# Spacing the turnings and reordering the join's side work in a chain of expert blocks

## The chip, the cores and the metric

The kernel runs on one core of one Trainium2 chip. The metric is the device time of one execution in microseconds (us). Unless said otherwise, times are medians of several executions. All executions of one comparison ran on the same chip.

## The reference, cut to what matters

```python
# first: a linear attention with a per-channel decay w, state (D x D) per head
for t in range(S):
    y[:, :, t] = einsum('bhd,bhde->bhe', rt, state + u*k*v)
    state = w * state + einsum('bhd,bhe->bhde', kt, vt)
# then: a mixture of 8 experts; x is the attention's output, (4*768, 384)
e = argmax(x @ w_gate)              # or the expert of the token before, if sigmoid(x @ w_local) >= 0.5
out[token] = softmax(logits)[e] * (relu(x[token] @ w1[e]) @ w2[e])     # 384 -> 1024 -> 384
```

Everything is float32. Each token goes to one expert, so the kernel sorts tokens by expert, gathers their rows, and works one block of rows for one expert at a time.

## The kernel before

The experts' part is a chain of ten blocks. Blocks 0 and 1 take 192 rows each. Blocks 2 to 9 take 448, 424, 392, 376, 352, 336, 232 and 192 rows. A block has eight hidden steps `m`; each is three matrix products with w1 (six matmul instructions in the trace), followed by ScalarE's relu into `hT`. Blocks of 336 rows and more ("seven") use a Strassen-like scheme on their first 256 rows: after every second hidden step, seven products instead of eight. VectorE prepares four `sums` of hT and four `factors` of w2 for them. At the block's end a `join` of seven VectorE operations puts the results together. The rows beyond 256 are the "rest" and have a PSUM bank of their own.

"Turning" means that TensorE transposes gathered rows into a PSUM bank and VectorE copies them out (`exT`). "Sending" is the way back: transposing the result `yT`, scaling it on VectorE, and scattering it. From block 2 on, both share one bank.

```python
def run(self, att, flag, ready):
    ...
    for i in range(n):
        u = self.units[i]
        if EARLY <= i and i + 1 < n:
            self.fetch(i + 1, self.nc.sync)
            self.gather(i + 1)
        after = len(self.units[i + 1]["rows"]) if i + 1 < n else 0
        for m in range(FK):
            self.hidden(i, m)
            ...
            if sends and (m >= 1 if i > EARLY else i == EARLY and m >= 4):
                self.send(*sends.pop(0))
            if u["seven"]:
                if m % 2:
                    self.sums(i, m // 2)
                    self.seven(i, m // 2)
                    if m < FK - 1:
                        self.factors(i, m // 2 + 1)
            elif m and i == n - 1:
                self.rows(m - 1)
            elif m:
                self.output(i, m - 1)
            if i <= EARLY:
                self.routing(i * FK + m)
            ...
            if FK - after <= m:
                self.turn(i + 1, m - (FK - after))
        if i + 1 < n and self.units[i + 1]["seven"]:
            self.factors(i + 1, 0)
            self.both = False
        if u["seven"]:
            self.join(i)
            ...

def join(self, i):
    ...                                        # p(k): product k in its bank
    nc.scalar.copy(one, p(1))
    nc.vector.tensor_tensor(u6, p(6), one, op=Alu.add)
    nc.vector.tensor_tensor(c[0][:, :half], p(2), one, op=Alu.add)
    ...                                        # four more
    nc.vector.tensor_tensor(c[0][:, half:], p(3), u6, op=Alu.add)
    for x in range(2):
        self.scaled(i, x, c[x], c[x])          # ScalarE: times the gate; then a scatter
    if n <= P or n == P + HALF:
        self.scaled(i, 2, u["y"][:, :D], ...)  # the rest bank, the same way
        ...
    else:
        nc.scalar.copy(u["yT"]..., u["y"]...)  # the rest bank, to be sent in the next block

def routing(self, s):                          # s counts hidden steps from block 0 on
    ...
    if s == 2 * FK:
        r.ends(bank("tb2"))                    # the router's end: 28 small VectorE operations
    if s == 2 * FK + 4:
        self.flag(bank("fp"))                  # the decay count: four VectorE ops, a 1x1 matmul, three more
```

There are two PSUM banks `h` for the hidden step, five `yo` tiles for results on the way out, and six tiles for gathered rows.

## Time and profile before

| | before |
|---|---|
| time, three executions | 410.75, 410.84, 412.0 us |
| span of the profiled execution | 408.3 us |
| TensorE, VectorE, ScalarE, GpSimd busy | 94, 47, 20, 35% |
| block 2's first hidden matmul starts | 155.58 us |
| last block's first half-row matmul starts | 398.06 us |

A row of the time order gives the start, the busy time, the engine, line, operation and tiles, and in brackets the idle time just ahead of it with what ended that. Read a row such as `[1.33 <-ACT hT L1066]` as a question: why did ScalarE make hT so late? The rows that carry the argument stand in the prediction.

### The profile page before, as it was taken

What the parts mean: (1) busy time and instruction counts of PE and PEld (TensorE: products, weight loads), DVE (VectorE), ACT (ScalarE), POOL (GpSimd) and SP (SyncE); (2) the same over time, 40 slices, a digit from 0 to 9 for tenths busy, and PEclk for the clock granted to TensorE, in tenths of its full rate; (3) what the DMA queues carried; (4) which work ended last, traced back from release to release, by engine and by line L of the source; (5) the groups of instructions that cost most, each with busy time, mean ns of one, the idle gap of its engine ahead of it and who ended that gap; (6) DMA issues with size and microseconds to landing.
All of it is one profiled execution on the core that took longest, in us unless ns stands there. A gap on an engine that the chain in (4) does not pass through costs nothing. (4 is left out here: it accounts for less than half of the span.)

```text
span 408.3 us, 8809 instructions
## 1 busy us (share of the span) xinstructions
PE 384.6 (94%) x3616; PEld 298.5 (73%) x3616; DVE 191.5 (47%) x533; ACT 80.4 (20%) x195; POOL 143.8 (35%) x179
## 2 busy tenths in 40 slices
PE   7999999999999999989899999989989989989992
PEld 6777787777779996656587767867757757769972
DVE  7887667788744616343332342462343344230201
ACT  4122322222222111111211121120130121121110
POOL 8679998874210250021150051033014004013011
PEclk9999999999999999999999999999999999999998
DMA  7999999994139847013630461172083072072011
GB/s 257 410 413 408 410 384 318 319 382 182 27 102 357 323 120 309 0 30 104 250 110 0 155 232 43 35 314 73 2 315 100 2 307 87 2 303 86 2 34 35
DMA packets 17473, 74.94 MB, mean 184 GB/s; under 512 B 2735, under 2 KB 6592, under 8 KB 14865
## 3 DMA queue, kind: packets, MB, share of 16 engines
q1 hardware_dynamic: 10048, 56.89, 36.4%
q0 software_dynamic: 3424, 9.54, 7.4%
q10 hardware_dynamic: 3952, 7.87, 5.2%
q8 instruction: 30, 0.49, 0.5%
q14 instruction: 19, 0.15, 0.1%
HBM read 64.85 MB, written 9.54 MB: 182 GB/s over the span
## 5 line engine op out<-in xcount | busy, mean ns | idle before, releaser
L1061 PE MATMUL h<-exT,w1t 128*128 128x192 f32 (+7 forms) x480 | 138.2, 429 | 2.9 <-DVE exT L1048 2.9
L1061 PEld LDWEIGHTS h<-exT,w1t 128*128 128x128 f32 x480 | 85.3, 190 | 35.6 <-issue 12.7
L1176 POOL DMA_INDIRECT out_dram<-yo,sid x27 | 27.0, 1001 | 197.6 <-ACT yo L1171 131.0
L1066 ACT ACTIVATE hT<-h 128x192 f32<-128x192 f32 (+6 forms) x64 | 26.8, 428 | 140.9 <-PE h L1061 140.9
L1048 DVE COPY exT<-tp 128x384 f32<-128x384 f32 (+7 forms) x29 | 14.3, 494 | 68.0 <-PE tp L1047 68.0
L1034 POOL DMA_INDIRECT xg<-x_d,gid x29 | 29.8, 1027 | 45.7 <-DVE sm L873 25.8
L1084 DVE TENSOR_TENSOR sums<-hT 128x128 f32<-128x128 f32 x40 | 11.5, 288 | 60.3 <-ACT hT L1066 60.3
L288 DVE TENSOR_TENSOR am<-pair,kept 128x768 f32<-128x768 f32 x32 | 30.1, 952 | 13.8 <-PE pair L286 13.3
L220 POOL TENSOR_TENSOR pd<-rk 128x384 f32<-128x384 f32 x32 | 31.7, 1011 | 3.1 <-PE y L267 2.1
L1074 PE MATMUL y<-hT,w2t 128*128 128x192 f32 (+1 forms) x144 | 29.3, 340 | 1.2 <-ACT hT L1066 1.2
L1106 PE MATMUL y<-factors,sums 128*128 128x192 f32 x144 | 27.4, 327 | 0.7 <-DVE sums L1084 0.7
L295 PE MATMUL y<-am,kv 128*64 128x128 f32 x384 | 27.3, 278 | 0.8 <-DVE y L271 0.6
L1074 PEld LDWEIGHTS y<-hT,w2t 128*128 128x128 f32 x144 | 24.9, 190 | 2.0 <-ACT hT L1066 1.6
L216 POOL TENSOR_TENSOR ke<-kv,endT 128x288 f32<-128x288 f32 x32 | 24.9, 796 | 4.2 <-DMA kv<-in_kv_dram 3.2
L233 POOL TENSOR_TENSOR rw<-rk,tab 128x384 f32<-128x384 f32 x26 | 23.5, 923 | 4.8 <-PE y L308 4.8
L295 PEld LDWEIGHTS y<-am,kv 128*64 128x64 f32 x384 | 23.6, 136 | 1.6 <-DVE y L271 1.2
L1106 PEld LDWEIGHTS y<-factors,sums 128*128 128x128 f32 x144 | 24.0, 190 | 1.0 <-DVE sums L1084 1.0
L286 PE MATMUL pair<-rw,kw 48*64 48x128 f32 (+1 forms) x768 | 22.5, 249 | 1.2 <-ACT end L167 0.6
L1113 PE MATMUL tp<-w2t,hT 128*120 128x384 f32 (+2 forms) x48 | 19.7, 491 | 2.8 <-ACT hT L1066 2.8
L286 PEld LDWEIGHTS pair<-rw,kw 48*64 48x64 f32 x768 | 19.4, 133 | 2.7 <-issue 1.0
L312 ACT COPY xT<-y 128x768 f32<-128x768 f32 (+1 forms) x16 | 12.5, 779 | 38.7 <-PE y L308 38.7
L1106 PE MATMUL y<-w2t,hT 128*128 128x192 f32 x80 | 19.6, 326 | 0.0
(255 smaller groups left out, 501.5 us busy)
## 6 DMA issues: line engine op xcount, KB each, us to landing
w1t<-in_w_dram SPq DMA_DIRECT2D x9, 1536.0 KB, 6.2
w2t<-in_w_dram SPq DMA_DIRECT2D x9, 1536.0 KB, 7.1
rk<-in_rk_dram SPq DMA_DIRECT2D x15, 768.0 KB, 9.7
kv<-in_kv_dram SPq DMA_DIRECT2D x16, 584.0 KB, 9.3
vT<-in_vT_dram SPq DMA_DIRECT2D x16, 384.0 KB, 7.7
x_d<-x ACTq DMA_DIRECT2D x4, 1152.0 KB, 9.3
w1t<-in_w_dram ACTq DMA_DIRECT2D x1, 1536.0 KB, 9.0
w2t<-in_w_dram ACTq DMA_DIRECT2D x1, 1536.0 KB, 12.3
```

Source lines behind the costliest of these rows:

```text
L216: nc.gpsimd.tensor_mul(t["ke"][:, p::2], t["k"][:, p::2], spread(self.endT[:, p, hp], 1, C2))
L220: nc.gpsimd.tensor_mul(t["pd"][:, z], t["rT"][:, z], t["kT"][:, z])
L233: engine.tensor_mul(t["rw"][:, z], t["rT"][:, z], spread(pw, 1, z.stop - z.start))
L286: nc.tensor.matmul(sc[f * DP:(f + 1) * DP, h, i, x:], lhsT=t["kw"][q, c, o * DP:(o + 1) * DP], rhs=t["rw"][q, c, x:], start=True, stop=True)
L288: return lambda: nc.vector.tensor_mul(t["am"][:, g], sc, spread(self.kept[:, g:g + 3], 1, 2))
L295: nc.tensor.matmul(t["y"][p * DP:(p + 1) * DP, h, c2 * P:(c2 + 1) * P], lhsT=t["v"][:, (2 * c + h) * DH:(2 * c + h) * DH + DP], rhs=t["am" ...
L1034: self.nc.gpsimd.indirect_dma_start(out=xg[:n], out_offset=None, in_=self.x_d[:rows], in_offset=bass.IndirectOffsetOnAxis(ap=u["gid"][:n, ...
L1061: nc.tensor.matmul(h[:, :n], lhsT=u["w1"][:, m, kk, :], rhs=u["xT"][:, kk, :], start=(kk == 0), stop=(kk == DK - 1))
L1066: nc.scalar.activation(u[m], h[:, :n], Act.Relu)
L1074: nc.tensor.matmul(u["y"][d][:, :n], lhsT=u["w2"][:, m, d * P:(d + 1) * P], rhs=u[m], start=(m == 0), stop=(m == FK - 1))
L1106: nc.tensor.matmul(bank[:, x * half:(x + 1) * half], lhsT=a, rhs=b, start=(j == 0 and x == 0), stop=(j == FK // 2 - 1), skip_group_check=True)
L1176: self.nc.gpsimd.indirect_dma_start(out=out.rearrange("n (h d) -> (n h) d", h=2) if half else out, out_offset=bass.IndirectOffsetOnAxis(ap ...
```

## The change

Its intent is to close TensorE's holes around the borders of the large blocks, without changing any arithmetic.

```diff
 # join: the rest bank is emptied first
         nc.scalar.copy(one, p(1))
+        if n <= P or n == P + HALF:
+            self.scaled(i, 2, u["y"][:, :D], ...)
+        else:
+            nc.scalar.copy(u["yT"]..., u["y"]...)
         nc.vector.tensor_tensor(u6, p(6), one, op=Alu.add)
 ...
         for x in range(2):
             self.scaled(i, x, c[x], c[x])
-        if n <= P or n == P + HALF:
-            self.scaled(i, 2, ...)
-        else: ...
 # routing: the decay count moves ahead and is split, the router's end moves back by a step
-        if s == 2 * FK:
-            r.ends(bank("tb2"))
-        if s == 2 * FK + 4:
-            self.flag(bank("fp"))
+        if s == 13:
+            self.flag(0)
+        if s == 14:
+            self.flag(1, bank("fp"))
+        if s == 2 * FK + 1:
+            r.ends(bank("tb2"))
+            self.flag(2)
 # run
-                self.gather(i + 1)                       # at the block's start
+            lag = 2 if i and self.units[i - 1]["seven"] and i < n - 1 else 1
             for m in range(FK):
                 self.hidden(i, m)
-                if sends and (m >= 1 if i > EARLY else i == EARLY and m >= 4):
-                    self.send(*sends.pop(0))
                 if u["seven"]:
-                    if m % 2:
+                    if m % 2 == 0:
+                        if sends and (i > EARLY or m >= 4):
+                            self.send(*sends.pop(0))
+                    else:
+                        if m // 2 >= FK // 2 - after:
+                            self.turn(i + 1, m // 2 - (FK // 2 - after))
                         self.sums(i, m // 2)
                         self.seven(i, m // 2)
 ...
+                else:
+                    if sends and m >= 1 and i > EARLY:
+                        self.send(*sends.pop(0))
 ...
-                elif m:
-                    self.output(i, m - 1)
+                    elif m >= lag:
+                        self.output(i, m - lag)
-                if FK - after <= m:
+                if not u["seven"] and FK - after <= m:
                     self.turn(i + 1, m - (FK - after))
-            if i + 1 < n and self.units[i + 1]["seven"]:
-                self.factors(i + 1, 0)
+            if EARLY <= i + 1 and i + 2 < n:
+                self.gather(i + 2)                       # at the block's end
             if u["seven"]:
                 self.join(i)
 ...
+            if i + 1 < n and self.units[i + 1]["seven"]:
+                self.factors(i + 1, 0)
```

## The prediction

> **What bounds the kernel now.** I read the page first, then the list of waits, then the order of time from 108 us on, for TensorE alone and for all engines around the block borders.
>
> ```profile
> span 408.3 us, 8809 instructions
> PE 384.6 (94%) x3616; PEld 298.5 (73%) x3616; DVE 191.5 (47%) x533; ACT 80.4 (20%) x195; POOL 143.8 (35%) x179
> PEclk9999999999999999999999999999999999999998
> ```
>
> TensorE (PE) is busy 94% at full clock; no other engine passes half. So the time is TensorE's stream plus its holes, and only the holes can be won, as the change keeps every matmul. The chain of waits on the page is only the last scatter (1 us) and says nothing, so I looked for holes directly. The experts' part starts at 117 us with two blocks of 192 rows. Then come six blocks with seven products (448 to 336 rows; I call them blocks 2 to 7, from 155.6 us to 362 us) and two small ones, 8 (232 rows) and 9. Each border between the large blocks looks like this one, from block 5 to 6:
>
> ```profile
> 299.46 0.41 PE L1047 MATMUL tp<-ident,xg 96*128 96x96 f32 x3
> 299.91 0.46 DVE L1048 COPY exT<-tp 128x288 f32<-128x288 f32 x1 [2.23 <-PE tp L1047]
> 300.29 0.35 DVE L1092 TENSOR_TENSOR factors<-w2t 128x192 f32<-128x192 f32 x1
> 300.43 3.82 PE L1061 MATMUL h<-exT,w1t 128*128 128x352 f32 x12 [0.55 <-DVE exT L1048]
> 301.49 0.35 DVE L1148 TENSOR_TENSOR t<-y,t 128x192 f32<-128x192 f32 x1
> 303.20 0.35 DVE L1154 TENSOR_TENSOR yo<-mp,t 128x192 f32<-128x192 f32 x1
> 303.58 1.12 ACT L1171 ACTIVATE yo<-yo,gate 128x384 f32<-128x384 f32 x2 [5.23 <-DVE yo L1154]
> 304.61 0.56 ACT L1171 ACTIVATE yo<-tp,gate 120x384 f32<-120x384 f32 x1
> 305.07 0.80 ACT L1066 ACTIVATE hT<-h 128x352 f32<-128x352 f32 x2
> 305.57 0.89 PE L1113 MATMUL tp<-w2t,hT 128*96 128x384 f32 x2 [1.33 <-ACT hT L1066]
> ...
> 316.33 3.71 PE L1061 MATMUL h<-exT,w1t 128*128 128x352 f32 x12
> 319.88 0.81 PE L1113 MATMUL tp<-w2t,hT 128*96 128x384 f32 x2
> ```
>
> (The last two lines are from TensorE's own order of time.) Two holes are to be seen. First, the block's last turning ends in an exT copy for which the next block's first matmul waits, 0.55 us. Second, VectorE makes four factors, then seven join operations; ScalarE scales two tiles, then empties the rest bank, and only then comes the first hT, for which TensorE waits 1.33 us. Undisturbed, twelve hidden matmuls take 3.55 us from start to start (316.33 to 319.88); here they took 5.14. I measure losses this way, start to start, since a hole in a pipelined stream costs more than its idle entry says.
>
> Block 2 has three more, and the border to block 8 a large one:
>
> ```profile
> 163.32 1.24 PE L1106 MATMUL y<-factors,sums 128*128 128x192 f32 x6 [0.69 <-DVE sums L1084]
> 176.79 0.19 PE L1429 MATMUL tp<-r_ones,some 128*1 128x1 f32 x2 [1.24 <-DVE some L1428]
> 177.22 0.55 PE L1047 MATMUL tp<-ident,xg 128*128 128x128 f32 x3 [0.24 <-DVE over L1430]
> 187.54 0.55 PE L1047 MATMUL tp<-ident,xg 128*128 128x128 f32 x3 [0.71 <-DVE yo L1221]
> 363.05 2.62 PE L1061 MATMUL h<-exT,w1t 128*128 128x232 f32 x12 [0.57 <-DVE exT L1048]
> 366.89 1.44 PE L1074 MATMUL y<-hT,w2t 128*128 128x232 f32 x6 [1.23 <-ACT hT L1066]
> ```
>
> In block 2 the sums come late because the router's end (some 35 small operations) stands ahead of them on VectorE; the decay count makes TensorE wait twice; and a turning right behind a sending needs the one turning bank that VectorE still reads.
>
> **What the Trainium skill says.** "Perfetto Trace Analysis", section Optimization Strategy: find the gaps on the engine that binds, ask which semaphore ends them, and let that dependency start sooner; this trace names exT, hT, sums and some. "PSUM — Partial Sum Buffer", section Engine vs sequencer instructions: the Vector and Scalar queues are strict FIFO and matmuls start in program order. The border above agrees: hT at 305.07 us needs nothing from the join, but stands behind 1.5 us of scaling. So the place in the queue is the cost, and moving instructions is worth time. The same page, section PSUM bank collisions: engines are to be kept apart by bank, which is why a turning waits 0.71 us for the yo read of the same bank.
>
> **The change part by part.** No operation is added or removed except by place; the built order shows the same TensorE instructions.
>
> Turnings apart: in seven-product blocks each turning now stands after an odd hidden step and before the sums and products. The last exT copy (0.46 us) lies under some 3.2 us of products, and a hidden step of 2 us separates each turning from a sending. This takes away the first hole: turning to first hidden, start to start, against 0.33 us in mid-block: 0.42 us (block 3), 0.29, 0.78, 0.65, 0.57, 0.70 (block 8), together 3.4. In block 2 it takes away 187.54 minus 186.34, less 0.33, so 0.9.
>
> Rest bank first, factors after the join: let M be the start of the last product (299.14 at the border shown). The join's first operation needs product 7, which ends near M+0.2. It took 2.09 us from there to ScalarE's first scaling (301.49 to 303.58) and 1.03 us for the two scalings. The emptied rest bank (0.46 us) moves ahead, where ScalarE is idle. So hT starts at M+3.3 instead of M+5.9, and TensorE can use it 0.5 us later, at M+3.8. TensorE itself comes there at M+0.33 plus twelve hidden matmuls: 4.27 us for 424 rows, 3.95, 3.79, 3.55, 3.39 (336), so at M+4.6 down to M+3.7. The wait is gone up to 352 rows and about 0.1 at 336. The losses before, twelve matmuls' start to start less those times and the 0.1 of refill behind them: 1.36, 0.91, 0.98, 1.68, 1.81 us, together 6.7. About 6.6 of it goes. For blocks 4 and 5 this includes the sending's wait for yT, whose copy now lies before the join.
>
> Block 8: with two outputs' lag the third hidden step comes before the first output. But there are two h banks, so that step waits for the same first hT. TensorE is there at M+0.33+2.34, that is M+2.7; the bank is free near M+3.7. I expect 1.05 us to stay of 1.61, so 0.55 won, and the lag itself worth nothing.
>
> Router's end and decay count: the count's test is made two steps ahead, so neither the matmul nor the turning behind it waits: 175.05 to 177.22 is 2.17 us, less 0.33 for the sending and 0.1 for the matmul, so 1.7. The router's end now stands behind the first sums: 163.32 minus 162.14, less 0.33, plus refill, 0.95. It took VectorE 4.8 us (158.15 to 162.98). In the new place exT and sums of the next step follow. TensorE gives 4.5 us of hidden work, 0.3 of turning and 2.3 us of products before it needs them, 7.1 against 4.8+0.6+0.3. It fits with some 1 us to spare.
>
> Gathers: they go to GpSimd before the join's scatters. Turnings now start at the second hidden step, but the gathers for block 3 ended at 151 us already, and later ones get a whole block. This is needed for the turnings and wins nothing.
>
> The sum: 3.4 + 0.9 + 6.6 + 0.55 + 1.7 + 0.95 = 14.1 us. All of it is on TensorE's stream, and nothing waits for something else than that stream between 155 and 398 us. 410.8 less 14.1 is 396.7; I add half a microsecond for waits not seen, 397.2 us, 3.3% less.
>
> **The rivals.** One: the wait moves instead of going. VectorE's order has exT ahead of sums, so a product could wait for its sums, above all in block 2 behind the router's end, and the join's scatters now follow three or four gathers of 1.3 us each (1.0 and a 0.3 gap), so a yo buffer could come free late. Against it: the sums have 2.3 us of products ahead of them, and the five yo buffers come round only after most of a block (over 20 us). It would leave 2 to 4 us, some 400 us. Two: the join chain stays the bound. If VectorE's first join operation had to wait for the last product (M+0.5) or the scalings slipped, each of blocks 6 to 8 would keep 0.3 to 0.5 us more, 398.5 us. Three: the holes were filled anyway, as weights or the clock bind. Against it: weight transfers land 7 us after issue in blocks of 30 us, and the clock is already full (0.996); TensorE shows no wait for a transfer in this part. It would give 408 us or more.
>
> **Range and chances.** The sum rests on durations from the trace, each with a few tenths of error, and more can go wrong than can go better than nearly all of the holes closed. So 395.2 to 400.5 us. 2% faster is 402.6 us, reached if 58% of the sum comes. Faster 0.94, within 2% 0.05, slower 0.01.
>
> **What would show it.** TensorE's waits should list no exT, no some or over, no yo and no sums of note; only hT at block 8 near 1 us, and perhaps 0.1 at block 7. TensorE busy stays 384 us or a little less while the span falls to about 395 us, and its share rises to 97%. At each border the first hT should start 3.3 us after the last product's start. I would be wrong if product 5 waits for sums in every large block, if TensorE waits for gathers at the second hidden step, or if hT still comes 5 us or more after the last product.

## The result, and the profile after

The changed kernel took 397.66 us (median of four executions, 396.65 to 398.36) beside 411.42 for the kernel before (four, 410.75 to 414.32). The ratio is 0.9651, with a 95% interval of 0.9597 to 0.9704. It is the mean time of one kernel's fast runs over that of the other's of the same rounds, so it is not quite the ratio of the two medians. Later, on another occasion and with more rounds, it was 0.9671 (0.9640 to 0.9702).

The head of the page, and TensorE's list of waits (total, times, longest; waits of 0.4 us and less left out):

```profile
span 396.6 us, 8820 instructions
...
PE 382.4 (96%) x3616; PEld 298.0 (75%) x3616; DVE 190.4 (48%) x533; ACT 81.1 (20%) x195; POOL 144.5 (36%) x179
```

```profile
PE pair L151 <- POOL ident masks.py:199: 1.6, 1, 1.6
PE y L308 <- issue: 1.2, 1, 1.2
PE h L1061 <- ACT hT L1066: 1.0, 1, 1.0
PE y L295 <- DVE y L271: 0.6, 2, 0.4
PE pair L286 <- ACT end L167: 0.6, 1, 0.6
```

TensorE's busy time is almost what it was (384.6 before); its holes are gone. Of the waits named in the prediction one is left, for hT at block 8. The others listed lie in the attention part, which the change does not touch. The border from block 5 to 6 now:

```profile
292.37 0.59 ACT L1172 ACTIVATE yo<-tp,gate 120x384 f32<-120x384 f32 x1
...
293.25 0.49 PE L1106 MATMUL mp<-w2t,sums 128*128 128x192 f32 x2
...
293.53 0.36 DVE L1154 TENSOR_TENSOR t<-y,t 128x192 f32<-128x192 f32 x1 [1.95 <-PE y L1106]
293.58 3.71 PE L1061 MATMUL h<-exT,w1t 128*128 128x352 f32 x12
...
295.25 0.34 DVE L1160 TENSOR_TENSOR yo<-mp,t 128x192 f32<-128x192 f32 x1
...
295.63 1.12 ACT L1172 ACTIVATE yo<-yo,gate 128x384 f32<-128x384 f32 x2 [2.67 <-DVE yo L1160]
...
296.65 0.44 ACT L1066 ACTIVATE hT<-h 128x352 f32<-128x352 f32 x1
...
297.15 0.89 PE L1113 MATMUL tp<-w2t,hT 128*96 128x384 f32 x2
```

The last product starts at 293.25 us, and the next block's hidden matmuls follow 0.33 us later with no turning between. The rest bank is emptied before the last product even starts. The first hT comes 3.40 us after the last product's start (5.93 before), and TensorE goes on at 297.15, which is 3.57 us after its first hidden matmul: undisturbed would be 3.55.

Block 8 keeps its hole:

```profile
351.67 2.51 PE L1061 MATMUL h<-exT,w1t 128*128 128x232 f32 x12
355.13 1.44 PE L1061 MATMUL h<-exT,w1t 128*128 128x232 f32 x6 [0.95 <-ACT hT L1066]
```

**A measure without the attention part.** Block 2 began at 155.58 us in the one trace of the kernel before and at 157.82 us in the first one of the changed kernel. In the thirteen traces it ranged from 155.58 to 163.72 us, although the attention code is the same in all. In the first pair 1.97 of the 2.24 us were there before any experts' code: TensorE stood idle for 1.24 us at 60 us and again near 73 us, for no wait that the profile shows. I therefore read the **stretch** from block 2's first hidden matmul to the last block's first half-row matmul: 242.48 us before (398.06 minus 155.58), 228.48 us after (386.30 minus 157.82), so 14.0 us less. The decay count's 1x1 matmul now stands just outside it and costs little: from the last of the summing matmuls to block 2 it is 9.46 us (148.36 to 157.82) against 9.19.

### The profile page after: what moved, and what is told of

Read it like the earlier page. It is cut to its first block, busy times and chain, and to the rows that moved or that the text cites.

```text
span 396.6 us, 8820 instructions
## 1 busy us (share of the span) xinstructions
PE 382.4 (96%) x3616; PEld 298.0 (75%) x3616; DVE 190.4 (48%) x533; ACT 81.1 (20%) x195; POOL 144.5 (36%) x179
## 5 line engine op out<-in xcount | busy, mean ns | idle before, releaser
L1106 PEld LDWEIGHTS y<-w2t,hT 128*128 128x128 f32 x80 | 14.2, 190 | 7.0 <-issue 2.7
```

What stands on the lines that cost most here:

```text
L1106: nc.tensor.matmul(bank[:, x * half:(x + 1) * half], lhsT=a, rhs=b, start=(j == 0 and x == 0), stop=(j == FK // 2 - 1), skip_group_check=True)
```

## The experiments

Eleven runs were made, ten variants and the changed kernel once more as a control, all with correct results. Whole times moved by 1% between occasions (the kernel before: 411.4 to 415.4 us), so each is compared as a ratio to the kernel before of its own occasion, and by the stretch of its one profiled execution.

| label | what it is | ratio to before (95%) | stretch us | against changed |
|---|---|---|---|---|
| (changed) | first traced run | 0.9651 (0.9597 to 0.9704) | 228.48 | |
| turns_at_end | turnings late | 0.9828 (0.9782 to 0.9874) | 233.72 | +5.24 |
| rest_last | rest bank emptied last | 0.9843 (0.9783 to 0.9902) | 235.47 | +6.99 |
| factors_first | factors ahead of the join | 0.9707 (0.9648 to 0.9766) | 228.48 | 0.00 |
| gathers_late | gathers behind the scatters | 0.9859 (0.9798 to 0.9920) | 234.80 | +6.32 |
| count_back | decay count in block 2 | 0.9712 (0.9675 to 0.9748) | 230.13 | +1.65 |
| ends_back | router's end a step sooner | 0.9700 (0.9671 to 0.9729) | 229.64 | +1.16 |
| lag_one | block 8 without the lag | 0.9653 (0.9610 to 0.9697) | 228.50 | +0.02 |
| turns_end_factors_first | two parts undone | 0.9881 (0.9842 to 0.9920) | 237.48 | +9.00 |
| after_again | changed kernel, control | 0.9671 (0.9640 to 0.9702) | 228.50 | +0.02 |
| scale_later | scalings behind two hT steps | 0.9626 (0.9587 to 0.9665) | 226.94 | -1.54 |
| scale_later_lag_one | the same without the lag | 0.9652 (0.9611 to 0.9693) | 226.93 | -1.55 |

The control repeats the stretch within 0.02 us, so differences of a few tenths in this column mean something, where the whole times cannot show them.

### Turnings late

```diff
-                        if m // 2 >= FK // 2 - after:
-                            self.turn(i + 1, m // 2 - (FK // 2 - after))
                         self.sums(i, m // 2)
...
-                if not u["seven"] and FK - after <= m:
+                if FK - after <= m:
                     self.turn(i + 1, m - (FK - after))
```

> The changed kernel with its turnings put back to the last four (or three, or two) hidden steps, behind the sums and products; all else as changed. My theory (the gains add, each hole is its own): the exT copy stands before each next block again, 3.4 us over six borders, and in block 2 the two sendings at steps 4 and 6 are again followed at once by a turning in the same bank, 0.87 us each, 1.7 us: 5.1 us slower than the changed kernel, some 402.5 us. TensorE lists about 2.9 us of idle ended by exT again. Rival (the join chain was the only real bound, the turnings free once it is short): under 1.5 us slower.

The stretch grew by 5.24 us. TensorE's order of time at the border from block 5 to 6:

```profile
300.63 0.41 PE L1047 MATMUL tp<-ident,xg 96*128 96x96 f32 x3
301.60 3.82 PE L1061 MATMUL h<-exT,w1t 128*128 128x352 f32 x12 [0.55 <-DVE exT L1048]
305.25 0.81 PE L1113 MATMUL tp<-w2t,hT 128*96 128x384 f32 x2
```

The exT hole is back, and no hT hole follows. The latter is worth a thought: the late copy delays the join too, but it delays TensorE's own arrival as much (the join starts 1.15 us after the last product's start instead of 0.28, the next hidden step 1.29 us after it instead of 0.33). The two clashes in block 2 were 0.71 and 0.70 us idle. My theory held.

### The rest bank emptied last

```diff
-        (the rest bank's emptying, ahead of the join's VectorE operations)
         for x in range(2):
             self.scaled(i, x, c[x], c[x])
+        (the rest bank's emptying)
```

> The changed kernel with the rest bank emptied after the two scalings again; turnings and factors as changed. My theory (the place in ScalarE's queue is the cost): hT starts 0.46 us later at each border, M+3.8 after the last product's start M instead of M+3.3. TensorE hardly notices in block 3; in blocks 4 and 5 the first sending waits for yT, ready near M+3.9 and wanted near M+2.3, 1.5 us each; blocks 6, 7 and 8 lose 0.3 to 0.5 us each. Together 4.3 us, some 402 us. Rival (ScalarE's order does not matter while VectorE's join is the longest piece): under 1 us.

The stretch grew by 6.99 us, where I expected 4.3. Its idle entries are 1.55 us (block 4's first sending), 1.90 (block 5's), 0.33 and 0.47 (hT in blocks 6 and 7), and 1.42 instead of 0.95 in block 8: 4.72 us more than the changed kernel's. So the places and nearly the sizes are as expected. Most of the rest is the clock. This view gives, for each stretch of 2 us, the busy time of each engine (TensorE first) and then the granted TensorE clock, as a share of full speed (the last two numbers are the DMA engines' busy share and GB/s):

```profile
270.00:272.00 2.00, 0.86 (x3) 0.19 (x1) 1.94 (x7) 0.79 (x2) 0.00 (x0) 1.00 0.76 231
272.00:274.00 2.00, 1.24 (x6) 0.96 (x7) 0.98 (x3) 1.10 (x3) 1.59 (x2) 0.98 0.94 350
274.00:276.00 2.00, 2.00 (x4) 1.00 (x3) 0.00 (x0) 0.00 (x0) 1.56 (x2) 0.50 0.88 293
276.00:278.00 2.00, 2.00 (x6) 1.17 (x5) 1.00 (x5) 0.48 (x1) 0.00 (x0) 0.67 0.63 257
278.00:280.00 2.00, 2.00 (x13) 1.83 (x12) 1.15 (x4) 0.00 (x0) 0.00 (x0) 1.00 0.04 15
```

The 1.90 us hole ended at 272.76 us:

```profile
272.24 0.48 ACT L1162 COPY yT<-tp 128x408 f32<-128x408 f32 x1
272.61 0.48 ACT L1066 ACTIVATE hT<-h 128x376 f32<-128x376 f32 x1
...
272.76 0.55 PE L1220 MATMUL tp<-ident,yT 128*128 128x128 f32 x3 [1.90 <-ACT yT L1162]
```

Soon after it the clock fell to half for some 3.4 us. That costs 2 times (0.02 + 0.50 + 0.33), 1.7 us. Holes of 4.72, the clock's 1.7 and, for what is left, 0.6 us that no idle entry shows make the 6.99. The Trainium skill describes such a gate ("TensorE: Matmul & The Clock Gate", section What's actually happening): half speed after at least one idle window of some 3.4 us, with windows that run freely. The halved clock and its length agree with this trace; the hole ahead of it was shorter than the page's window.

The clock records in the traces show the windows themselves. In this trace the clock is halved from 151.05 us on (after a hole of 1.92 us that the edit does not touch), from 273.93 us on, and from 403.63 us on, after TensorE's last matmul; the first two times for 3.41 us. The starts are 122.88 and 129.70 us apart, 36 and 38 times 3.413 us, so the windows do run on whatever the kernel does. Laid over the holes, the 1.92 and the 1.90 us hole each lie wholly in the window just before a halving (147.63 to 151.05, 270.52 to 273.93). In another run (the scalings moved, without the lag, below) a hole of 1.93 us at 148 us falls across the border of two windows, 1.44 us in one and 0.50 in the next, and the clock stays full. So whether a hole of this size costs 1.7 us more is partly chance. The median alone hides this: two of the four executions had a mean clock of 0.986 (409.81 and 409.28 us) and two of 0.994 to 0.995 (405.89 and 406.40); two halvings of 3.41 us in 408 us take 0.008 off the mean.

### Factors ahead of the join

```diff
+            if i + 1 < n and self.units[i + 1]["seven"]:
+                self.factors(i + 1, 0)
+                self.both = False
             if EARLY <= i + 1 and i + 2 < n:
                 self.gather(i + 2)
             if u["seven"]:
                 self.join(i)
...
-            (the same three lines here)
```

> The changed kernel with the next block's first four factors ahead of the join on VectorE again (1.08 us); turnings and rest bank as changed. My theory: the join, the scalings and hT come 1.08 us later, hT usable at M+4.9. Block 3 has slack (its 32 half matmuls lie between). Blocks 4 and 5 lose 0.3 and 0.45 us, block 6 about 1.0, block 7 about 1.2, block 8 nothing (no factors stand ahead of it): 2.9 us, some 400.5 us. Rival (the factors lie beside other work): under 1 us; then TensorE shows no wait on hT in blocks 6 and 7.

This was a clear miss: the stretch is the same to a hundredth. VectorE's order of time shows why:

```profile
292.05 0.28 DVE L1084 TENSOR_TENSOR sums<-hT,sums 128x128 f32<-128x128 f32 x1
292.25 0.35 DVE L1092 TENSOR_TENSOR factors<-w2t 128x192 f32<-128x192 f32 x1
...
293.18 0.35 DVE L1092 TENSOR_TENSOR factors<-factors,w2t 128x192 f32<-128x192 f32 x1
294.28 0.36 DVE L1154 TENSOR_TENSOR t<-y,t 128x192 f32<-128x192 f32 x1 [0.75 <-PE y L1106]
```

The factors need only w2, which has long been there. They follow the last sums at once, in time in which VectorE waits for product 7 anyway, and are done 0.75 us before it. In the kernel before they could not, as the late turning's exT copy stood ahead of them in the queue and itself waited for TensorE.

### Gathers behind the scatters

```diff
                 self.fetch(i + 1, self.nc.sync)
+                self.gather(i + 1)
...
-            if EARLY <= i + 1 and i + 2 < n:
-                self.gather(i + 2)
```

> The changed kernel with the gathers at the start of the block before again, so behind the join's scatters on GpSimd. My theory: only block 3 suffers, since its first turning for block 4 stands at the second hidden step: four scatters end near 200.7 us, a gather lands 3 to 4.5 us after its start, the turning stood at 199.9 us, so one wait of 4 to 5 us, ended by a transfer, and nothing elsewhere: some 402 us. Rival (the gathers' place is cosmetic, turnings have the slack): no difference from the changed kernel, 397.7 us.

The stretch grew by 6.32 us, most of it in one place of block 3:

```profile
203.70 2.30 PE L1061 MATMUL h<-exT,w1t 128*128 128x424 f32 x6
209.93 0.52 PE L1047 MATMUL tp<-ident,xg 128*128 128x128 f32 x3 [3.93 <-DMA xg<-x_d,gid]
```

GpSimd's order shows the queue that did it: four scatters (the last two are shown), then the gather that was wanted.

```profile
203.96 0.98 POOL L1177 DMA_INDIRECT out_dram<-yo,sid  x1 [0.30 <-issue]
205.25 0.98 POOL L1177 DMA_INDIRECT out_dram<-yo,sidh  x1 [0.30 <-issue]
206.54 1.07 POOL L1034 DMA_INDIRECT xg<-x_d,gid  x1 [0.31 <-issue]
```

A second wait of 0.29 us stands in block 6, which I had not expected, and after the 3.93 us hole the clock was halved again (0.83 mean over the 10 us from 210 us on, so 1.7 us). Thus 3.93, 0.29 and 1.7 make 5.9 of the 6.32 us. The gathers' place wins nothing by itself, but the early turnings need it.

### Decay count and router's end

```diff
 # count_back
-        if s == 13: self.flag(0)
-        if s == 14: self.flag(1, bank("fp"))
+        if s == 2 * FK + 4: self.flag(0); self.flag(1, bank("fp")); self.flag(2)
 # ends_back
-        if s == 2 * FK + 1:
+        if s == 2 * FK:
             r.ends(bank("tb2"))
```

> The changed kernel with the decay count's test, matmul and reading back at step 4 of block 2, behind that step's sending; all else as changed. From here on I compare the stretch from block 2's first hidden matmul to the last block's first half-row matmul, read from TensorE's order of time: 242.48 us before, 228.48 us changed, 228.48 with factors first, 233.72 with the turnings at the end. My theory: one wait of 1.2 us for the test behind the sending's yo on VectorE, 1.4 us longer with the refill, 229.9 us; no turning stands behind it now, so the second wait of 0.24 us does not return. Rival (the count costs its matmul wherever it stands): under 0.3 us.

> The changed kernel with the router's end back at the first step of block 2, so ahead of the first exT copy and sums on VectorE. My theory: VectorE is busy with it from about 2.4 us to 7.2 us after the block's start, then 0.6 us of exT copy, so the first sum is ready near 8.2 us, while TensorE wants it near 7.2 us: a wait of 0.9 to 1.3 us for sums, 229.6 us for the stretch. Rival (now that no other wait stands in block 2 the slack swallows it): no wait, 228.5 us.

The stretch grew by 1.65 and 1.16 us, where 1.4 and 1.1 were expected. One row of each kernel's time order:

```profile
178.39 0.19 PE L1446 MATMUL tp<-r_ones,some 128*1 128x1 f32 x2 [1.25 <-DVE some L1444]
```

```profile
166.16 1.08 PE L1106 MATMUL y<-factors,sums 128*128 128x192 f32 x5 [0.88 <-DVE sums L1084]
```

Both holes return where they were said to. Of the 1.65 us, 0.27 is the count's matmul itself, which has moved back into the stretch (ahead of block 2 it is 9.19 us again instead of 9.46), so 1.38 net. A 1x1 matmul with 0.19 us of work costs that much when its operand comes from a VectorE that has just been given something else to do.

### Block 8 without the lag

```diff
-            lag = 2 if i and self.units[i - 1]["seven"] and i < n - 1 else 1
+            lag = 1
```

> The changed kernel with the outputs of block 8 one step behind the hidden ones as everywhere else. My theory (two h banks: the third hidden step needs the first hT just as the first output does, so the lag buys nothing): the wait of 0.95 us moves from the third hidden step to the first output, the stretch stays 228.5 us within 0.1. Rival (the lag hides a hidden step of 1.17 us): 0.5 to 1.2 us longer.

The wait moved to the output matmul and kept its size, and the stretch stayed (228.50):

```profile
350.46 2.51 PE L1061 MATMUL h<-exT,w1t 128*128 128x232 f32 x12
353.94 1.44 PE L1074 MATMUL y<-hT,w2t 128*128 128x232 f32 x6 [0.96 <-ACT hT L1066]
```

More independent work ahead of a wait helps only where it has somewhere to put its result. With two banks, a third hidden step waits for the same ScalarE step.

### Turnings late and factors first together

The edit is that of both experiments above.

> Turnings at the end and factors ahead of the join, both put back at once. Factors first alone cost nothing (228.48 us), where I had expected 2.9: with the turnings early, VectorE makes the factors in idle time before the last product ends. Revised theory: they only stand in the way behind the exT copy of a late turning. Then here the join comes 1.08 us later than with the turnings at the end alone: block 6 waits 1.0 us more for hT, block 7 1.2, blocks 3 to 5 0.3 to 0.5 each, block 8 nothing: 233.72 + 3.5 = 237.2 us. Rival (the place of the factors never matters, VectorE makes them early or late without harm): 233.7 us.

The stretch was 237.48 us, within 0.3 of the revised theory and 3.8 us off its rival. At the border from block 5 to 6:

```profile
297.23 0.46 DVE L1048 COPY exT<-tp 128x288 f32<-128x288 f32 x1 [2.23 <-PE tp L1047]
297.61 0.35 DVE L1092 TENSOR_TENSOR factors<-w2t 128x192 f32<-128x192 f32 x1
...
298.81 0.35 DVE L1154 TENSOR_TENSOR t<-y,t 128x192 f32<-128x192 f32 x1
...
302.42 0.89 PE L1113 MATMUL tp<-w2t,hT 128*96 128x384 f32 x2 [0.86 <-ACT hT L1066]
```

So the factors cost 3.76 us (237.48 minus 233.72) with late turnings and nothing with early ones. Either edit cures them; together they are worth 9.00 us, more than the 5.24 and 0.00 that they cost when undone singly.

### The scalings behind two hT steps, with and without the lag

The wait left in block 8 suggests one more move of the same sort: ScalarE's two scalings of the join are needed by nobody on TensorE's path, so let the next block's first two hT steps go ahead of them.

```diff
 # join
-        for x in range(2):
-            self.scaled(i, x, c[x], c[x])
-        if n == P + HALF: ...
+        self.later = lambda: self.joined(i, c)          # the same lines, called from run
 # run
                 self.hidden(i, m)
+                if m == 1 and self.later:
+                    self.later()
+                    self.later = None
```

> The changed kernel again, as the control for the two next runs on the same chip: 0.965 of the kernel before, stretch 228.5 us, one wait of 0.95 us at block 8.

> The changed kernel with the join's two scalings (and the half rows' one in block 2) put behind the next block's first two hT steps on ScalarE, so that hT no longer stands behind the join. My theory: the last wait goes at block 8, 0.95 us and 0.1 of refill: stretch 227.4 us, no TensorE wait in it, 1.0 us faster than the control. Rival (the wait comes back further on: the third hT stands behind 1.0 us of scaling, or a scatter comes late for its yo buffer): stretch 228.0 to 229 us with a new wait on hT or yo.

> The same with block 8's outputs one step behind. My theory: with no wait left the lag is still worth nothing: 227.4 us within 0.1. Rival: the second output waits for a second hT that stands ahead of the scalings only by a little, 0.2 to 0.6 us longer than with the lag.

The stretch fell to 226.94 us with the lag and 226.93 without, 1.56 us below the control, and TensorE has no wait left in it. In the first of the two, at block 8 (ScalarE and TensorE rows):

```profile
354.95 0.37 ACT L1066 ACTIVATE hT<-h 128x232 f32<-128x232 f32 x1 [2.06 <-issue]
...
356.12 0.36 ACT L1066 ACTIVATE hT<-h 128x232 f32<-128x232 f32 x1 [0.81 <-PE h L1061]
356.38 1.11 ACT L1177 ACTIVATE yo<-yo,gate 128x384 f32<-128x384 f32 x2
...
357.05 1.34 PE L1074 MATMUL y<-hT,w2t 128*128 128x232 f32 x6
```

I had expected 1.05. About 0.3 more stood in blocks 6 and 7, where hT came so narrowly that the stream lost a few hundredths to 0.16 us without an idle entry (323.02 to 326.57 us in the changed kernel is 3.55 against 3.39). In whole time the median was 398.72 against the control's 400.99 on the same chip, but the two ratios' intervals overlap, so the trace shows the gain and the timing alone does not prove it. In the whole times of the variant without the lag (0.9652) nothing of it is to be seen: its six executions spread from 397.77 (the profiled one) to 402.10, and the three slowest had mean clocks of 0.985 to 0.993, the other three of 0.994 to 0.997. Only the profiled one can be looked into.

## Why the prediction was right

The prediction named 397.2 us and the result was 397.66. That they are within half a microsecond is partly luck, since the four executions alone spread over 1.7 us; the stretch, free of most of that, is the better test. By its own steps:

- **Turnings apart, 3.4 + 0.9 us.** Right. Undone alone it cost 5.24 us, of which 1.7 had been expected for two clashes in block 2 (there was only one such clash in the kernel before, as the count's wait hid the other). Less the second clash's 0.87 it is 4.4, against the 4.3 named.
- **Rest bank first, factors after the join, 6.6 us.** The size was right: the holes at the five borders are gone, with 0.02 us left at 352 rows and 0.16 at 336 (0.1 was named) and 0.07 of refill behind each, so 6.4 us went. The first hT came 3.40 us after the last product's start, 3.3 named. But the credit within the term was misplaced. Taking the 1.08 us of factors off the path was put down to their move behind the join; the run showed this move worth 0.00 in the changed kernel. The turning's move does it already, since it takes the exT copy from in front of them. I had held VectorE's order fixed where the change had altered what VectorE waits for. The sum did not suffer, as both moves were made at once.
- **Block 8, 0.55 us, and the lag worth nothing.** Right about the lag, which when taken out moved the wait but not the time, and about the cause; the gain was a little smaller. 355.13 minus 351.67, less 2.34, leaves 1.12 us where 1.05 was named; with 0.1 of refill, which the 1.61 before includes, 1.22 stayed, so 0.39 was won.
- **Decay count 1.7, router's end 0.95.** Right about the places. Undone, they cost 1.65 and 1.16 us. The 1.65 is not quite the 1.7 of the prediction: it includes the 0.27 us of moved matmul, and of the two waits before only the first came back, since no turning stands behind it now. (The router's end is 28 operations in the trace, not the prediction's 35; its 4.8 us are right.)
- **Gathers: needed, worth nothing themselves.** Right, and understated: late, they cost 6.32 us, over a quarter of it through the clock.
- **The sum, 14.1 us.** The stretch is shorter by 14.0 us. The half microsecond that I added for waits not seen cannot be checked: the added matmul outside the stretch took 0.27 us of it, and the attention part varies by more than the rest.
- **The rivals.** No product waits for sums in the changed kernel and no turning for a gather, so the wait did not move. The join chain stayed the last bound, by 0.02 and 0.16 us at blocks 6 and 7 and by 1.1 us at block 8, until its scalings were moved as well. The clock and the weights did not bind: within the stretch the changed kernel's trace shows the full clock throughout and no TensorE wait for a transfer.
- **What would show it.** TensorE's share rose to 96%, not the 97% named, since the span came out 396.6 us and not 395.

The parts are not additive, and the experiments say so: undone singly they cost 5.24, 6.99, 0.00, 1.65 and 1.16 us (the gathers aside), 15.0 us in all, against 14.0 for the whole. The rest bank's 6.99 includes 1.7 of clock (13.3 without it), and the two that share a queue are worth 9.00 together.

What stays open: why block 2 starts anywhere from 155.6 to 163.7 us in traces whose earlier code is the same. Single holes of 0.3 to 1.9 us, near 60, 73, 113 and 148 us among others, belong to it, most of them with nothing that the profile shows being waited for. In the two latest starts (162.28 and 163.72 us) a halved clock after a hole of 1.92 us adds 1.7. No run here was made to settle it.

## What to carry to other kernels

When one engine is nearly full, list its holes, measure each from start to start against the same piece undisturbed, and ask for each which engine's queue stood in the way rather than which operation is slow; here 14 us came from moving instructions, with none removed. Put work that nobody waits for behind work that the full engine waits for, and put anything that itself waits for the full engine behind what is ready, because in a first-in first-out queue it holds up all that follows. Undo parts in pairs as well as singly: a part that costs nothing when undone alone may only be covered by another.

## What the Trainium skill lacked or had wrong

- "TensorE: Matmul & The Clock Gate", section What's actually happening, gives an idle window of some 3.4 us as what sends the clock to half, and does not say how much of the window must be idle. Here part of one was enough. With the windows laid out from the halvings, the four halvings in the middle of a kernel (two with the rest bank last, two with the gathers late) each follow a window in which TensorE's records leave 1.87, 1.90, 1.92 and 2.30 us idle; windows with up to 1.66 us idle were not followed by one in any of the thirteen traces. The limit is not exact: one window at the end of a kernel (the router's end a step sooner, from 388.90 us on) had 1.95 us idle and no halving behind it. Each of the four lasted 3.41 us and cost 1.7 us, nearly as much as the hole.
- "Perfetto Trace Analysis", section Optimization Strategy, says to find the gaps, not that the idle entry understates the loss. Between 155 and 398 us the idle entries of the kernel before sum to 12.0 us and those of the changed one to 0.95, a difference of 11.1; the stretch differs by 14.0, of which 0.27 is the count's matmul that left it. With 15 entries fewer, that is about 0.2 us more for each hole than it shows.
- No page gives a size for TensorE's standing idle with no wait shown, as it does in the attention part: 1.24 us in the first trace of the changed kernel, up to 1.66 (turnings late, at 74.6 us). If the traces' matmuls and weight loads are counted in order of start, such holes of over 0.3 us stand before the same numbers in different traces: 1217 in four, 2241 in three, 2753 in eight. These are 1024 and 512 apart, multiples of 256. The point may belong to "Runtime: NRT & Kernel Launch", section Instruction fetch mechanics; what causes the holes, no run here tested.
